# Order and size of loads around batch 1 of a sorted-block attention and its bilinear layer, with output tiles in halves

## The chip, the cores and the metric

One Trainium2 chip, one of its cores. The time is the device time of one execution in microseconds, as the median of several executions. Before the change it is 246.88 us (median of 3 runs, 246.43 to 246.95). A profile is taken from one further execution.

The engines have the profile's names: PE multiplies matrices (PEld loads its stationary operand), DVE and ACT work elementwise, POOL does that too and issues the loads, SP (SyncE) issues transposing DMAs and stores. All of them run their own list of instructions in order and wait for each other through semaphores.

## The reference

Four batches, eight heads, 768 positions, head size 64, blocks of 96 positions (8 blocks). Weights: 512 x 1536 twice and 1536 x 512. Inputs and output are float32.

```python
P = sort_net                                   # (4, 8, 8, 8)
for _ in range(5):
    P = exp(P - max(P, -1));  P = P / sum(P, -1);  P = P / sum(P, -2)
k_sorted = einsum('bhij,bhjcd->bhicd', P, k_blocks)
v_sorted = einsum('bhij,bhjcd->bhicd', P, v_blocks)
attn = softmax(q_blocks @ k_sorted^T / 8)      # inside each block
x = (attn @ v_sorted) -> (3072, 512)           # heads side by side
out = ((x @ w_a) * (x @ w_b)) @ w_out          # (3072, 512)
```

## The kernel before

**Units of work.** A *pair* is two heads of one batch; pairs 0 to 3 are batch 0, 4 to 7 batch 1, 8 to 11 batch 2, 12 to 15 batch 3. For each pair, k and v of all blocks are mixed by P (`pair_mix`, tiles kT and vT), v is turned by a transposing DMA of SP (`turn_v`, tile vs), q is brought into order by POOL (`pair_q`, tile qc, two buffers) and turned by a DMA of SP (`turn_q`, tile qTf, three buffers). Then come the scores and their exponential (`pair_scores`, tile eT), and the output of attention with its scaling on DVE (`pair_o` with `one_o`, tile xp), which SP turns into xT, the input of the bilinear layer. Batch 0 is done in another way, in two halves and with PE's own transposes, to begin early.

**The bilinear layer.** For each batch `ffn_ab(b, m, t)` computes one of 12 strips m of 128 columns for one half t of the batch's positions: four products with w_a, four with w_b, a copy by ACT, and the elementwise product by DVE into hT. Then `ffn_out(b, c)` computes one of six output tiles of 128 rows: 12 products with w_out into one PSUM tile, a copy by ACT or DVE, a store by SP.

**How they are laid between each other.** PE works on the bilinear layer of batch b, and the attention of batch b+1 lies between its steps. `units_full(b+1)` gives 12 units in the order M0 M1 R0 M2 R1 O0 M3 R2 O1 R3 O2 O3, where M is mixing and turning, R the scores and O the output of a pair. `interleave` runs the steps and after each of them as many units as keep up with the steps' count; an output tile counts as two steps (`outs`). The manual schedule keeps every engine's instructions in the order in which this program issues them.

**PSUM.** The attention's tiles (mix, sc, o_ps) share the two buffers of psA, the bilinear layer's (pf, po) the four of psF.

**The loads.** All loads are issued by POOL into one queue, cast from float32 to bfloat16 on the way; one issue takes POOL about 0.73 us. An issue waits until the load eight places earlier has landed. The order before is: q of batch 0, k and v of pairs 0 to 3, six chunks of 256 columns of w_a and w_b (`load_ab`), pairs 4 and 5, three chunks of w_out, pairs 6 and 7. A pair's load is three DMAs (k, v, q; 192 KB each as written). Between them POOL spreads P into the form that the mixing takes (`spread`, 2.0 us for a batch's heads) and copies pair 4's q. Pairs 8 and 9 are loaded in `pair_o` of pairs 6 and 7 (L311 to L316), pairs 10 and 11 in M of pairs 8 and 9 (L420), pairs 12 to 15 in `pair_o` of pairs 8 to 11. The pairs' tiles have six buffers (`ld`), so that pair 8 takes those of pair 2.

**SP's queue.** It carries the turns and the stores in program order. Around the end of batch 0 that is: turns of q and v of pairs 4 to 7 alternating, xT of pair 4, v of pair 7, then stores of output tile 0, xT of pair 5, stores of tile 1, xT of pair 6, stores of tile 2, q of pair 8, xT of pair 7, stores of tiles 3 to 5.

The steps of the prediction touch L108 to L117 (loads of weights), L263 to L272 (`pair_q`, `turn_q`), L309 to L323 (`pair_o`), L372 to L379 (`ffn_out`), L415 to L440 (`units_full`, `interleave`), and L551 to L572 (the order of the loads and the first two stretches of steps).

Of the kernel before, what the change touches and what calls it, by code (L numbers as in the profile page):

```python
# [9 lines left out]
FP32 = mybir.dt.float32  # L10
BF16 = mybir.dt.bfloat16
# [11 lines left out]
def kernel(  # L23
# [11 lines left out]
    nc = tc.nc  # L35
    P = 128
    B, H, S, D = q.shape
# [3 lines left out]
    DMODEL = H * D  # L41
# [4 lines left out]
    NCH = S // P  # L46
    HP = H // 2
    NPAIR = B * HP
    KA = DMODEL // P
    KO = DFF // P  # L50
    KH = KO // 2
# [6 lines left out]
    V0 = 16  # L58
    W = NCH * D
    HW = S // 2  # L60
    WC = 256
    NBUF = 3
    PSUM = bass.MemoryType.PSUM
    ET = mybir.EngineType
# [1 line left out]
    const = ctx.enter_context(tc.tile_pool(name="const", bufs=1))  # L66
# [5 lines left out]
    outp = ctx.enter_context(tc.tile_pool(name="outp", bufs=1))  # L72
    psA = ctx.enter_context(tc.tile_pool(name="psA", bufs=2, space=PSUM))
    psF = ctx.enter_context(tc.tile_pool(name="psF", bufs=4, space=PSUM))
# [18 lines left out]
    def load_pair(g):  # L93
        base = 2 * g * S * D
        tiles = []
        for name, t in (("k2", k), ("v2", v), ("q2", q)):
            if g < HP and name == "q2":
                continue
            to = ld.tile([P, 2, W], BF16, tag=name, name=name)
            nc.gpsimd.dma_start(out=to, in_=_ap(t, base, [[W, P], [S * D, 2], [1, W]]))  # L100
            tiles.append(to)
        loaded[g] = tiles
# [3 lines left out]
    w_out_sb = const.tile([P, KO, DMODEL], BF16, name="w_out_sb")  # L106

    def load_ab(c):  # L108
        for w_ap, w_sb in ((moe_w_a, w_a_sb), (moe_w_b, w_b_sb)):
            nc.gpsimd.dma_start(  # L110
                out=w_sb[:, :, c * WC:(c + 1) * WC],
                in_=w_ap.rearrange("(kc p) n -> p kc n", p=P)[:, :, c * WC:(c + 1) * WC])

    def load_out(c):
        nc.gpsimd.dma_start(
            out=w_out_sb[:, c * 4:(c + 1) * 4, :],
            in_=moe_w_out.rearrange("(kc p) n -> p kc n", p=P)[:, c * 4:(c + 1) * 4, :])  # L117
# [6 lines left out]
    for c in range(2):  # L124
        load_ab(c)
# [4 lines left out]
    kTs = [const.tile([P, S + PAD], BF16, name=f"kT{n}") for n in range(NBUF)]  # L130
# [23 lines left out]
    p_col = const.tile([P, NB, BH], BF16, name="p_col")  # L154

    def spread(eng, src, h0, n, i0=0, ni=NB):
        eng.tensor_tensor(
            out=s_all[:, h0:h0 + n, i0:i0 + ni],
            in0=_ap(mask, 0, [[CG, P], [0, n], [0, ni], [1, CG]]),
            in1=_ap(src, i0 * BH + h0, [[NB * BH, P], [1, n], [BH, ni], [0, CG]]),  # L160
            op=ALU.mult)

    def copy(eng, out, in_):
        if eng == "act":
            nc.scalar.copy(out=out, in_=in_)  # L165
        else:
            nc.vector.tensor_copy(out=out, in_=in_)  # L167
# [92 lines left out]

    def pair_q(g):  # L263
        qc = qtp.tile([P, NCH, 2, D], BF16, tag="qc", name="qc", bufs=2)
        nc.gpsimd.tensor_copy(out=qc.rearrange("p c e d -> p e c d"),  # L265
                              in_=loaded[g][2].rearrange("p e (c d) -> p e c d", c=NCH))
        st[g, "qc"] = qc

    def turn_q(g):
        qT = qtp.tile([P, NCH, P], BF16, tag="qTf", name="qTf", bufs=3)  # L270
        nc.sync.dma_start_transpose(out=qT, in_=st[g, "qc"].rearrange("p c e d -> p (c e d)"))
        st[g, "qT"] = qT  # L272
# [35 lines left out]

    def pair_o(g):  # L309
        xp = att.tile([BLK, NB, 2, D], BF16, tag="xp", name="xp")  # L310
        if g == 2 * HP - 2:  # L311
            load_pair(2 * HP)
        elif g == 2 * HP - 1:
            load_pair(2 * HP + 1)
            pair_q(2 * HP)
            turn_q(2 * HP)  # L316
        elif g >= 2 * HP and g + HP < NPAIR:
            load_pair(g + HP)
        for hf in range(2):
            one_o(eTs[g % NBUF], hf, vss[g % NBUF], hf * NBH, xp, NB)  # L320
        nc.sync.dma_start_transpose(
            out=xT_of(g // HP)[:, g % HP, :].rearrange("p (i t) -> p i t", i=NB),
            in_=xp.rearrange("p i e d -> p (i e d)"))  # L323

    hTs = {}
# [32 lines left out]
    def store(b, c, o):  # L360
        if b == 0:
            h, u = divmod(c, 3)
            for c2 in range(2):
                nc.sync.dma_start(
                    out=_ap(out, (h * PH * NCH + 2 * u + c2) * DMODEL,
                            [[NCH * DMODEL, PH], [1, DMODEL]]),
                    in_=o[c2 * PH:(c2 + 1) * PH])
        else:
            rows = out[b * S:(b + 1) * S, :].rearrange("(p c) n -> c p n", c=NCH)
            nc.sync.dma_start(out=rows[c], in_=o)  # L370

    def ffn_out(b, c):  # L372
        po = psF.tile([P, DMODEL], FP32, tag="F", name="po")
        for m in range(KO):
            nc.tensor.matmul(po, lhsT=hTs[b][:, m, c * P:(c + 1) * P], rhs=w_out_sb[:, m, :],  # L375
                             start=(m == 0), stop=(m == KO - 1))
        o_sb = outp.tile([P, DMODEL], FP32, tag="o_sb", name="o_sb", bufs=3)
        copy("act" if c % 2 == 0 else "dve", o_sb, po)
        store(b, c, o_sb)  # L379

    def ffn_out_cut(b, c, cut):
        rows = out[b * S:(b + 1) * S, :].rearrange("(p c) n -> c p n", c=NCH)[c]
        for n0, n1, eng, queue in ((0, cut, "dve", nc.sync), (cut, DMODEL, "act", nc.scalar)):
            po = psF.tile([P, DMODEL], FP32, tag="F", name="po")
            for m in range(KO):
                nc.tensor.matmul(po[:, 0:n1 - n0], lhsT=hTs[b][:, m, c * P:(c + 1) * P],  # L386
                                 rhs=w_out_sb[:, m, n0:n1],
                                 start=(m == 0), stop=(m == KO - 1))
            o_sb = outp.tile([P, n1 - n0], FP32, tag=f"o_cut{n0}", name="o_cut")
            copy(eng, o_sb, po[:, 0:n1 - n0])  # L390
            queue.dma_start(out=rows[:, n0:n1], in_=o_sb)
# [23 lines left out]
    def units_full(b):  # L415
        def M(g):
            pair_mix(g, "k", ("act", "act"))
            pair_mix(g, "v", ("dve", "act"))
            turn_v(g)
            if g in (2 * HP, 2 * HP + 1):  # L420
                load_pair(g + 2)
            if g + 1 < NPAIR and g + 1 != 2 * HP:
                pair_q(g + 1)
                turn_q(g + 1)

        g0 = b * HP
        order = [("M", 0), ("M", 1), ("R", 0), ("M", 2), ("R", 1), ("O", 0), ("M", 3),
                 ("R", 2), ("O", 1), ("R", 3), ("O", 2), ("O", 3)]
        what = {"M": M, "R": pair_scores, "O": pair_o}
        return [lambda w=w, n=n: what[w](g0 + n) for w, n in order]  # L430

    def interleave(steps, units, spare, slow=0, outs=0):
        n, done, at = len(steps), 0, 0
        for s, step in enumerate(steps):
            step()
            at += 1 if s < n - outs else 2
            want = s + 1 if s < slow else -(-at * len(units) // (n + outs - spare))
            while done < min(want, len(units)):
                units[done]()
                done += 1  # L440

    with tc.manual_schedule(engines={ET.PE, ET.Pool, ET.SP, ET.Activation, ET.DVE}):
        if True:
# [22 lines left out]
            for it in range(5):  # L466
                rsum, csum = chain[0][it], chain[1][it]
                nc.scalar.activation(out=p_nat, in_=p_nat, func=AF.Exp)
                if it == 2:
                    with nc.allow_low_precision("sum of one one and zeros"):  # L470
                        nc.vector.reduce_sum(
                            out=mask, in_=_ap(ident, 0, [[P, P], [1, CG], [CG, NB]]),
# [14 lines left out]
                else:  # L487
                    nc.vector.tensor_mul(
                        out=p_fin.bitcast(BF16).rearrange("h (i j u) -> h i j u", i=NB, j=NB),
# [58 lines left out]
                    half_x(0, 3, "act")  # L548
                ab_mms(begun[n], w_sb, 0, m, 0, range(KA - 1))

        load_ab(4)  # L551
        load_ab(5)
        load_pair(4)
        spread(nc.gpsimd, p_col, 8, 8)
        load_pair(5)
        for c in range(3):
            load_out(c)
        load_pair(6)
        pair_q(HP)
        turn_q(HP)  # L560
        load_pair(7)
        for n in range(2, 4):
            spread(nc.gpsimd, p_col, n * 8, 8)

        steps = [lambda: ffn_ab(0, 0, 0, begun[0:2]), lambda: ffn_ab(0, 1, 0, begun[2:4]),
                 lambda: ffn_ab(0, 2, 0, begun[4:5])]
        steps += [lambda m=m: ffn_ab(0, m, 0) for m in range(3, KO)]
        interleave(steps, units_half(), 1, 3)

        steps = [lambda m=m: ffn_ab(0, m, 1) for m in range(KO)]  # L570
        steps += [lambda c=c: ffn_out(0, c) for c in range(NCH)]
        interleave(steps, units_full(1), 6, outs=NCH)  # L572

        for b in range(1, B):
            steps = [lambda m=m, t=t, b=b: ffn_ab(b, m, t)
                     for m in range(KO) for t in range(2)]
            steps += [lambda c=c, b=b: ffn_out(b, c) for c in range(NCH)]
            if b == B - 1:
                steps[-1] = lambda b=b: ffn_out_cut(b, NCH - 1, 3 * P)
            interleave(steps, units_full(b + 1) if b + 1 < B else [], 8, outs=NCH)  # L580


# [28 lines left out]
```

## Time and profile before

| | us |
|---|---|
| median of 3 runs (range) | 246.88 (246.43 to 246.95) |
| the profiled execution | 247.89 |
| its span, first to last instruction | 246.1 |
| PE busy in it | 234.1 |
| DVE, ACT, POOL busy | 108.9, 104.0, 61.2 |
| share of 16 DMA engines' span: loads (queue 0), SP's DMAs (queue 1) | 40.9%, 29.6% |

The granted clock of PE was full in the whole span (mean 1.000). The page's second part cuts the span into 40 slices and gives the busy share of each in tenths; the list of waits gives, for each engine and line, what it waited for with the total, the number of times and the longest; the chain of waits goes back from the last instruction to what released it. In the rows of the DMA queues stand the packets that began in a window, their megabytes as written, and the time they took as a share of 16 engines' time in the window (over 100% where an engine has several packets in flight).

Where batches lie: batch 0's second half of positions is at 45 to 66 us with most of batch 1's attention between its steps, batch 0's output tiles at 66 to 85, batch 1's layer at 85 to 142, and so on to the last output tile at 243.

### The profile page before, as it was taken

Reading aid. Unit: us, or ns where it says so; the run is one execution under the profiler, and the core shown is the slowest. Engines: PE = TensorE matmul, PEld = TensorE weight load, DVE = VectorE, ACT = ScalarE, POOL = GpSimd, SP = SyncE. Lnnn points to the kernel's source line nnn. Section 1 sums busy time; section 2 is a strip of 40 time slices with the busy share of each in tenths; the row PEclk is TensorE's granted clock in tenths of the full one; section 3 lists DMA queues with packets and bytes.
Section 4 is the critical chain, followed back from the end, with each engine's and each line's share of the span. In section 5 each row is a group of like instructions: output and inputs, shape, how many; then the busy total and the mean of one; then the engine's idle time right before and its main releaser. Section 6 shows DMA issues by size and latency. Waiting matters only on the chain.

```text
span 246.1 us, 5514 instructions
## 1 busy us (share of the span) xinstructions
PE 234.1 (95%) x2250; PEld 139.2 (57%) x2259; DVE 108.9 (44%) x255; ACT 104.0 (42%) x204; POOL 61.2 (25%) x82
## 2 busy tenths in 40 slices
PE   6799999998979979999999999999999999999994
PEld 6576666665545446666654465666654466665443
DVE  6774557534426144464652153363561244443110
ACT  3575754674630047546430056737420033333001
POOL 8876857616144014471100001000000000000000
PEclk9999999999999999999999999999999999999999
DMA  6999999999999979899714335312114210000132
GB/s 80 203 199 194 196 201 206 167 185 168 149 113 235 207 180 119 147 157 192 115 23 128 131 91 105 75 34 43 35 44 149 85 45 0 0 3 1 43 123 90
DMA packets 56585, 28.67 MB, mean 117 GB/s; under 512 B 33392, under 2 KB 53616, under 8 KB 56560
## 3 DMA queue, kind: packets, MB, share of 16 engines
q0 software_dynamic: 20944, 14.16, 40.9%
q1 hardware_dynamic: 35472, 14.11, 29.6%
q8 instruction: 17, 0.28, 0.5%
q14 instruction: 8, 0.07, 0.1%
q10 hardware_dynamic: 144, 0.07, 0.1%
HBM read 28.32 MB, written 6.29 MB: 141 GB/s over the span
## 4 chain that ended last, share of the span: by engine, by line
PE 85%; DMA 7%; DVE 4%; ACT 1%; issue 1%; SPq 0%; DVEq 0%
PE pf L336 48%; PE po L375 22%; DMA qTf<-qc 3%; PE mix L281 3%; PE o_ps L249 3%; DMA xT<-xp 3%; PE sc L301 2%; PE mixh L199 2%; PE po L386 1%; PE vs_ps L226 1%; PE xt_ps L240 1%; PE sc L214 1%; DMA p_nat<-in_sort_net_dram 1%; PE two L336 1%; DVE xp L255 1%
## 5 line engine op out<-in xcount | busy, mean ns | idle before, releaser
L357 DVE TENSOR_TENSOR hT<-a_sb,pf 128x384 bf16<-128x384 bf16 x95 | 52.6, 554 | 77.0 <-PE pf L336 45.3
L336 PE MATMUL pf<-xT,w_a_sb 128*128 128x384 bf16 x380 | 78.0, 327 | 1.6 <-DMA xT<-xp 1.6
L336 PE MATMUL pf<-xT,w_b_sb 128*128 128x384 bf16 x380 | 77.4, 326 | 0.0
L356 ACT CAST a_sb<-pf 128x384 bf16<-128x384 f32 x95 | 45.5, 479 | 60.2 <-PE pf L336 38.9
L375 PE MATMUL po<-w_out_sb,hT 128*128 128x512 bf16 x267 | 60.6, 379 | 0.5
L336 PEld LDWEIGHTS <-w_b_sb 128*128 128x128 bf16 x384 | 37.5, 98 | 27.0 <-issue 2.4
L336 PEld LDWEIGHTS <-w_a_sb 128*128 128x128 bf16 x384 | 34.7, 98 | 22.2
L375 PEld LDWEIGHTS <-hT 128*128 128x128 bf16 x276 | 26.5, 98 | 30.8
L265 POOL COPY qc<-q 128x768 bf16<-128x768 bf16 x12 | 9.9, 826 | 77.3 <-DMA qTf<-qc 58.4
L165 ACT COPY o_sb<-po 128x512 f32<-128x512 f32 x12 | 7.0, 586 | 50.2 <-PE po L375 35.4
L167 DVE COPY o_sb<-po 128x512 f32<-128x512 f32 x11 | 7.6, 692 | 38.8 <-PE po L375 24.6
L306 ACT ACTIVATE eT<-sc 96x768 bf16<-96x768 f32 x24 | 18.2, 802 | 6.2 <-PE sc L301 6.2
L255 DVE TENSOR_TENSOR xp<-o_ps,rec 96x512 bf16<-96x512 f32 x24 | 16.5, 686 | 0.8
L165 ACT CAST kT<-mix 128x384 bf16<-128x384 f32 x24 | 10.3, 482 | 6.7 <-PE mix L281 6.7
L100 POOL DMA_DIRECT2D v<-in_v_dram x16 | 11.7, 729 | 1.9 <-PE pf L336 0.6
L100 POOL DMA_DIRECT2D k<-in_k_dram x16 | 11.7, 728 | 1.2 <-DMA w_a_sb<-in_moe_w_a_dram 0.6
L249 PEld LDWEIGHTS <-eT 96*128 96x128 bf16 x256 | 10.4, 97 | 2.6
L249 PE MATMUL o_ps<-vs,eT 96*128 96x65 bf16 x256 | 11.2, 193 | 0.0
L100 POOL DMA_DIRECT2D q<-in_q_dram x12 | 8.8, 734 | 1.9 <-DMA w_out_sb<-in_moe_w_out_dram 1.3
L253 DVE RECIPROCAL rec<-o_ps 96x8 f32<-96x8 f32 x32 | 6.3, 196 | 5.9 <-PE o_ps L249 5.9
L301 PE MATMUL sc<-qTf,kT 64*128 64x96 bf16 x192 | 6.3, 204 | 2.0 <-DVE xp L255 1.3
L301 PEld LDWEIGHTS <-kT 64*128 64x128 bf16 x192 | 4.5, 94 | 5.8 <-issue 3.2
(76 smaller groups left out, 147.6 us busy)
## 6 DMA issues: line engine op xcount, KB each, us to landing
out_dram<-o_sb SPq DMA_DIRECT2D x17, 256.0 KB, 2.0
k<-in_k_dram POOLq DMA_DIRECT2D x16, 192.0 KB, 7.8
v<-in_v_dram POOLq DMA_DIRECT2D x16, 192.0 KB, 8.1
q<-in_q_dram POOLq DMA_DIRECT2D x12, 192.0 KB, 9.0
w_a_sb<-in_moe_w_a_dram POOLq DMA_DIRECT2D x6, 256.0 KB, 9.8
w_b_sb<-in_moe_w_b_dram POOLq DMA_DIRECT2D x6, 256.0 KB, 10.1
w_out_sb<-in_moe_w_out_dram POOLq DMA_DIRECT2D x3, 512.0 KB, 12.3
out_dram<-o_sb SPq DMA_DIRECT2D x12, 128.0 KB, 4.3
```

The lines of the kernel that those rows point to most:

```text
L100: nc.gpsimd.dma_start(out=to, in_=_ap(t, base, [[W, P], [S * D, 2], [1, W]]))
L165: nc.scalar.copy(out=out, in_=in_)
L167: nc.vector.tensor_copy(out=out, in_=in_)
L249: nc.tensor.matmul(o_ps[:, e, i * (D + 1):(i + 1) * (D + 1)], lhsT=eT[:, hf, e, i * BLK:i * BLK + P], rhs=vs[0:BLK, i0 + i, V0 - 1 + e * ( ...
L255: nc.vector.tensor_tensor(out=_ap(xp, i0 * 2 * D, [[nxp * 2 * D, BLK], [D, 2], [2 * D, NBH], [1, D]]), in0=_ap(o_ps, 1, [[1024, BLK], [511 ...
L265: nc.gpsimd.tensor_copy(out=qc.rearrange("p c e d -> p e c d"), in_=loaded[g][2].rearrange("p e (c d) -> p e c d", c=NCH))
L301: nc.tensor.matmul(sc[:, e, i * BLK:(i + 1) * BLK], lhsT=kT[e * D:(e + 1) * D, blk * BLK:blk * BLK + P], rhs=qT[e * D:(e + 1) * D, :, blk ...
L306: nc.scalar.activation(out=eT[:, hf, :, 0:HB], in_=sc[0:BLK, :, 0:HB], func=AF.Exp, scale=float(scale))
L336: nc.tensor.matmul(pf[:, 0:HW], lhsT=w_sb[:, kc, m * P:(m + 1) * P], rhs=x_cols(b, kc, t), start=(kc == 0), stop=(kc == KA - 1))
L356: nc.scalar.copy(out=a_sb, in_=pf[:, 0:HW])
L357: nc.vector.tensor_mul(out=hT[:, m, t * HW:(t + 1) * HW], in0=a_sb, in1=ab[1][:, 0:HW])
L375: nc.tensor.matmul(po, lhsT=hTs[b][:, m, c * P:(c + 1) * P], rhs=w_out_sb[:, m, :], start=(m == 0), stop=(m == KO - 1))
```

## The change

1. The weights' columns are loaded in chunks of 256, 256, 512 and 512 (the first two before, the last two where the third and fourth were); the fifth and sixth chunk go.
2. The three chunks of w_out are loaded after pairs 6 and 7, not before them.
3. The spreads of P for batches 2 and 3 move from before the stretch into M of pairs 5 and 7.
4. Pairs 8 and 9 are loaded in M of pairs 6 and 7, which on POOL stand right after w_out.
5. Pairs 10 and 11 are held: POOL first copies one element (`hold`) of xp of pair 7, or of kT of pair 8, and issues the load after it.
6. q of pair 8 is copied and turned in `pair_o` of pair 5, not of pair 7. The loads in `pair_o` come after its output and turn.
7. Each output tile is two steps of six products; the weight of two steps for a whole tile (`outs`) goes. The last tile of all stays as it was.

As the program issues them, PE's instructions then differ in one stretch alone, batch 0's output tiles: pair 5's O stands after the first half of tile 0, pair 7's R after its second half, pair 6's O after tile 1, and pair 7's O after the first half of tile 2. Before, pair 5's O and pair 7's R both stood after tile 0, pair 6's O after tile 1, pair 7's O after tile 2. SP's order becomes: xT of pair 5, q of pair 8, stores of tiles 0 and 1, xT of pairs 6 and 7, stores of tiles 2 to 5.

```diff
-    WC = 256
+    AB = (0, 256, 512, 1024, 1536)
...
-                out=w_sb[:, :, c * WC:(c + 1) * WC],
-                in_=w_ap.rearrange("(kc p) n -> p kc n", p=P)[:, :, c * WC:(c + 1) * WC])
+                out=w_sb[:, :, AB[c]:AB[c + 1]],
+                in_=w_ap.rearrange("(kc p) n -> p kc n", p=P)[:, :, AB[c]:AB[c + 1]])
...
+    held = const.tile([1, 1], BF16, name="held")
+
+    def hold(of):
+        nc.gpsimd.tensor_copy(out=held, in_=of)
...
     def pair_o(g):
         xp = att.tile([BLK, NB, 2, D], BF16, tag="xp", name="xp")
-        if g == 2 * HP - 2:
-            load_pair(2 * HP)
-        elif g == 2 * HP - 1:
-            load_pair(2 * HP + 1)
-            pair_q(2 * HP)
-            turn_q(2 * HP)
-        elif g >= 2 * HP and g + HP < NPAIR:
-            load_pair(g + HP)
...
+        if g == HP + 1:
+            pair_q(2 * HP)
+            turn_q(2 * HP)
+        if g == 2 * HP - 1:
+            hold(xp[0:1, 0, 0, 0:1])
+            load_pair(2 * HP + 2)
+        elif g >= 2 * HP and g + HP < NPAIR:
+            load_pair(g + HP)
...
-        po = psF.tile([P, DMODEL], FP32, tag="F", name="po")
-        for m in range(KO):
-            nc.tensor.matmul(po, ...)
+        def part1():
+            v["po"] = psF.tile([P, DMODEL], FP32, tag="F", name="po")
+            mms(range(KH))
+
+        def part2():
+            mms(range(KH, KO))
...
-            if g in (2 * HP, 2 * HP + 1):
+            if g in (HP + 2, HP + 3):
                 load_pair(g + 2)
+            if g == 2 * HP:
+                hold(kTs[g % NBUF][0:1, 0:1])
+                load_pair(g + 3)
+            if g in (HP + 1, HP + 3):
+                spread(nc.gpsimd, p_col, (g - HP + 3) // 2 * 8, 8)
...
-        load_ab(4)
-        load_ab(5)
         load_pair(4)
         spread(nc.gpsimd, p_col, 8, 8)
         load_pair(5)
-        for c in range(3):
-            load_out(c)
         load_pair(6)
         pair_q(HP)
         turn_q(HP)
         load_pair(7)
-        for n in range(2, 4):
-            spread(nc.gpsimd, p_col, n * 8, 8)
+        for c in range(3):
+            load_out(c)
```

More of the change, by code (lines that the diff above doesn't have):

```diff
@@ L372, in ffn_out, with mms @@
     def ffn_out(b, c):
-        po = psF.tile([P, DMODEL], FP32, tag="F", name="po")
-        for m in range(KO):
[L375 to L379, printed above, removed]
+        v = {}
+        def mms(ms):
+            for m in ms:
+                nc.tensor.matmul(v["po"], lhsT=hTs[b][:, m, c * P:(c + 1) * P],
+                                 rhs=w_out_sb[:, m, :], start=(m == 0), stop=(m == KO - 1))
+        def part1():
[3 more added lines that the diff above has]
+            mms(range(KH, KO))
+            o_sb = outp.tile([P, DMODEL], FP32, tag="o_sb", name="o_sb", bufs=3)
+            copy("act" if c % 2 == 0 else "dve", o_sb, v["po"])
+            store(b, c, o_sb)
+        return [part1, part2]
     def ffn_out_cut(b, c, cut):
@@ L430, in units_full, with interleave @@
         return [lambda w=w, n=n: what[w](g0 + n) for w, n in order]
-    def interleave(steps, units, spare, slow=0, outs=0):
-        n, done, at = len(steps), 0, 0
+    def interleave(steps, units, spare, slow=0):
+        n, done = len(steps), 0
         for s, step in enumerate(steps):
             step()
-            at += 1 if s < n - outs else 2
-            want = s + 1 if s < slow else -(-at * len(units) // (n + outs - spare))
+            want = s + 1 if s < slow else -(-(s + 1) * len(units) // (n - spare))
             while done < min(want, len(units)):
@@ L570 @@
         steps = [lambda m=m: ffn_ab(0, m, 1) for m in range(KO)]
-        steps += [lambda c=c: ffn_out(0, c) for c in range(NCH)]
-        interleave(steps, units_full(1), 6, outs=NCH)
+        steps += [part for c in range(NCH) for part in ffn_out(0, c)]
+        interleave(steps, units_full(1), 6)
         for b in range(1, B):
@@ L576 @@
                      for m in range(KO) for t in range(2)]
-            steps += [lambda c=c, b=b: ffn_out(b, c) for c in range(NCH)]
+            steps += [part for c in range(NCH - (b == B - 1)) for part in ffn_out(b, c)]
             if b == B - 1:
-                steps[-1] = lambda b=b: ffn_out_cut(b, NCH - 1, 3 * P)
-            interleave(steps, units_full(b + 1) if b + 1 < B else [], 8, outs=NCH)
+                steps.append(lambda b=b: ffn_out_cut(b, NCH - 1, 3 * P))
+            interleave(steps, units_full(b + 1) if b + 1 < B else [], 8)
 _INS = ['q', 'k', 'v', 'sort_net', 'moe_w_a', 'moe_w_b', 'moe_w_out']
```

## The prediction

> **What bounds the kernel now.** I read the page first, then TensorE's waits, then the chain of waits from 44 to 92 us, and last the two DMA queues in short windows of that stretch.
>
> ```profile
> PE 234.1 (95%) x2250; PEld 139.2 (57%) x2259; DVE 108.9 (44%) x255; ACT 104.0 (42%) x204; POOL 61.2 (25%) x82
> PE   6799999998979979999999999999999999999994
> DMA  6999999999999979899714335312114210000132
> ```
>
> TensorE (PE) is busy for 234.1 of 246.1 us and its slices of 6.15 us are full from the sixteenth (92 us) to the last but one, so after that there is nothing that a schedule can win. The holes are at both ends, which the change leaves alone, and in the tenth, twelfth and fifteenth slice (55 to 92 us). The DMA row is nearly full until there. PE's own waits there:
>
> ```profile
> PE pf L336 <- DMA xT<-xp: 1.6, 1, 1.6
> PE sc L301 <- DVE xp L255: 1.3, 2, 0.8
> PE sc L301 <- DMA qTf<-qc: 0.8, 1, 0.8
> ```
>
> 3.7 us in three places; that is the most that the change can win. The chain of waits (start, length, what) places them:
>
> ```profile
> 48.62 8.47 DMA qTf<-qc
> 57.09 0.14 issue
> 57.23 0.52 PE sc L301 x16
> ...
> 68.88 0.26 PE o_ps L249 x8
> ...
> 70.24 0.70 DVE xp L255
> ...
> 70.98 0.34 PE sc L301 x8
> ...
> 80.94 6.49 DMA xT<-xp
> 87.48 0.97 PE pf L336 x5
> ```
>
> Wait A: the scores of pair 5 (57.23) stand 0.77 us for the turn of pair 5's q. Wait B: the scores of pair 7 (70.15 and 70.98) stand 0.77 + 0.49 us because pair 5's output step went right before them and holds both psA buffers until VectorE has scaled it. Wait C: batch 1's first product stands 1.62 us for the turn of pair 7's xp.
>
> The turns are DMAs of SyncE (queue 1); the loads are POOL's (queue 0). The lines below are queue rows (packets, MB, share of 16 engines) of the windows 20-22, 39-42, 49-51, 51.5-53.5 (two rows), 59-60, 44.5-46 (two rows), in this order:
>
> ```profile
> q0 software_dynamic: 784, 0.39, 144.8%
> ...
> q0 software_dynamic: 622, 0.62, 124.4%
> ...
> q0 software_dynamic: 555, 0.40, 131.2%
> ...
> q0 software_dynamic: 386, 0.28, 90.2%
> q1 hardware_dynamic: 385, 0.10, 36.5%
> ...
> q1 hardware_dynamic: 1068, 0.27, 126.2%
> ...
> q0 software_dynamic: 127, 0.13, 99.8%
> q1 hardware_dynamic: 121, 0.03, 55.0%
> ```
>
> Alone, queue 0 moves 0.20 MB a us and queue 1 1068 packets a us. Together they alternate packet for packet, 193 a us each: a turn of q or x (768 packets of 256 bytes) takes 4.0 us instead of 0.7 while loads are queued. And from 44.5 to 46 both nearly stop, after a load of code at 43.7. Loads of code at 26.9 and 34.1, with no turn in flight, show no such pause; those at 56.9, 69.9 and 81.2, with turns in flight, are followed by one of about 1 us each.
>
> **The change, part by part.** The order of PE's instructions differs in one place only, the first four output tiles of batch 0; ACT's and DVE's orders are the same. The whole effect thus lies in the three waits, or in new ones.
>
> *Half tiles (wait B).* After the change pair 5's output step comes after 6 of the 12 products of tile 0, and 6 more stand between it and pair 7's scores. In the chain the second psA buffer came free 70.98 - 68.68 = 2.30 us after the output step began. Now PE has the step (0.49), 6 products at 2.59/12 = 0.216 (1.30), 0.11 for entering a new group (7 products after scores took 1.62, not 1.51) and the first scores (0.23): 2.13. Left are 0.17 of waiting and 0.11 for the added boundary: 1.26 becomes 0.28, a gain of 1.0. Worst case 0.5, if pair 7's turn of q, which took 10.4 us from issue to landing, is late here; before, it had two pairs' loads beside it, after, one.
>
> *Pairs 10 and 11 held, pair 8's q turned early, half tiles (wait C).* Before, the last turn of xp was issued at 80.94, though xp was ready at 79.15: SyncE was issuing pair 8's turn of q (79.16, 1.69) that stood ahead of it. It landed 10.5 us after pair 7's output step began (76.94), and 8.9 were to be had. Now pair 8's turn is ahead of tiles 0 and 1's stores, and that step comes 6 products earlier against the rest: 0.49 + 42 x 0.216 + 0.11 + 3 x 0.163 = 10.1 us. The turn is issued 2.3 after the step begins. It takes 2.8 us (the fastest turn of q, alone), 6.5 (its own row) or 9.0 (pair 6's): landing at 5.1, 8.8 or 11.3, a wait of 0, 0 or 1.2. Pair 10's loads do not go away: the hold releases them once xp's first half is written, 1.5 us after the step begins, so they start beside this very turn. I take 0.3, a gain of 1.3 (0.4 to 1.6). The early turn makes SyncE wait for POOL's copy of pair 8's q, with the stores and turns of tiles 0 and 1, pairs 6 and 7 queued behind; POOL reaches it some 64 us in (after pair 5's turn lands: a copy 0.8, three issues 2.2, a spread 2.0, a copy 0.8), SyncE at 71: 7 us of cover.
>
> *w_out behind pairs 6 and 7, pair 8 right behind it (wait A).* The bytes up to w_out and pair 7 are the same, so their end stays near 55.5, where queue 0 ran dry before. What is new is pair 8. POOL issues it once pair 4's turn of q has landed (two qc buffers; 49.5 before, earlier now), so it stands in queue 0 with no gap: 3 x 256 packets, 768/193 = 4.0 us more of alternation, and the turns of pair 4's v and pair 5's q (1024 + 768 packets, issued at 47.34 and 48.62, behind the same vT as before) have to live with it. Before, they ended in the gap after 55.5. Credits: (a) wider chunks move 2.1 MB at 0.207 MB a us (the window 39-42 row, 1 KB packets) instead of 0.196: 0.57 us or 0.115 MB, 150 of pair 8's packets, 0.8 us. (b) Pair 4's turn of q lies beside 768-byte packets instead of 1 KB ones (146 a us at 43-44): some 0.075 MB less is held up, 0.5 us. (c) That turn now starts about 2 us earlier and is through by 44.6, so the pause of 44.5 finds no turn: 1.5 us at 0.20 instead of 0.13 MB, 0.17 MB, 1.15 us. Left: 4.0 - 0.8 - 0.5 - 1.15 = 1.55 us longer. In that time queue 1 has 300 of its own packets moved (0.28 us alone): the turn lands 1.3 later, at 58.4, and wait A grows by 1.3. Upper bound: no credits (4.0 less 0.7, 3.3) and a pause at 57.4 on the unfinished turn (1.0): 4.3. Lower bound: pair 8 comes too late to matter and the credits stand: the wait is gone, -0.8. I take +1.3, nearest to the rows of this stretch.
>
> [...] The trace has 0.196 against 0.207, which is why I keep (a).
>
> *Costed at nothing.* Wide chunks land later as wholes: the b half of the first by 27.5 (its last narrow part before), needed at 30.3. w_out lands near 54, needed at 66.1; were that cover gone, each us would count. Spreads (2.0 each) move into POOL's idle stretches. The hold before pair 11 keeps POOL until kT of pair 8 (90); behind it pair 9's q has until 103.4. Pairs 12 to 15 come up to 4 us later; the next to use one is batch 3, at 141.7.
>
> **Sum.** -1.0 (B) - 1.3 (C) + 1.3 (A) = -1.0, rounded down to -0.9 for small boundaries. The profiled span of 246.1 becomes 245.2, with the 1.8 around it 247.0. The profiled execution took 247.89, the median of the runs is 246.88; against the median: 246.0.
>
> **Rivals.** *Pair 8 holds up the turns (slower).* One mechanism, at wait A: for it speak the alternation row and the three pauses that met turns; against it, credits (a) to (c). Without (c) and with the pause at 57.4: (4.0 - 1.3) x 0.82 (1.3 of 1.55, as above) + 1.0 = 3.2, so 3.2 - 1.0 - 1.2 = +1.0: 247.9; without any credit +2.0: 248.9. It decides from a landing of 59.9 on. *The pause alone (no change):* credits stand, the pause strikes: 2.3 - 1.0 - 1.3 = 0: 246.9. Measured, 0.2% (0.5 us) either way can't be told from no change. *Pair 8 comes late:* wait A vanishes, 246.9 - 0.8 - 2.3 = 243.8; against it: pair 4's turn has to land before 51.0 for its own scores.
>
> **How the numbers follow.** Forecast 0.39, late pair 8 0.07, the pause alone 0.18, held up 0.36. The first two are faster by over 0.2%: 0.46; same 0.18; slower 0.36. The forecast's own range is 245.0 to 246.4 (A between +0.5 and +1.7). The range for 8 in 10: 244.5 (a little of the late-pair case) to 248.5 (most of the slower one).
>
> **What would show it.** Wait B under 0.4; wait C under 0.5; pair 5's turn of q landing at 58.4, and pair 8's loads issued before 50. A landing past 59.9 makes the forecast wrong and the slower rival right; a wait for w_out, or PE waits after 92 us, would be something that I have not seen.

## The result, and the profile after

| | before | after |
|---|---|---|
| median of 4 runs each (range) | 246.91 (246.43 to 247.18) | 250.83 (249.89 to 251.4) |
| ratio, 95% interval | | 1.0157 [1.0122, 1.0192] |
| profiled execution | 247.89 | 250.68 |
| its span | 246.1 | 248.9 |
| mean granted clock of PE | 1.000 | 0.986 |

The changed kernel is slower by 1.6%, 3.9 us. The forecast (246.0) is wrong, and 250.83 lies 2.3 us above the end of the range, 248.5. Here and below a median is that of all runs, and a ratio leaves out single slow runs, those over 1.5% above their kernel's fastest.

First the page of the changed kernel: PE's busy time, its 40 slices of 6.2 us, and the clock that was granted to it in the same slices.

```profile
PE 237.9 (96%) x2250; PEld 141.6 (57%) x2259; DVE 109.0 (44%) x255; ACT 103.9 (42%) x204; POOL 58.7 (24%) x80
...
PE   7899999994999999999999999999999999999994
...
PEclk9999999996799999999999999999999999999999
```

PE is busy for 237.9 us where it was busy for 234.1, with the same 2250 matmuls. Most of that is work at a lower clock (2.64 of the 3.8 us, below), and the last row says where: slices ten and eleven, 56 to 68 us. It had a full clock everywhere before.

PE's waits (total, times, longest) that answer to the three of before:

```profile
PE sc L306 <- DMA qTf<-qc: 3.6, 1, 3.6
...
PE o_ps L249 <- DVE xp L255: 0.4, 1, 0.4
```

Wait B (scores of pair 7) and wait C (batch 1's first product) are gone, and a new one of 0.42 us stands at the output step of pair 7. Wait A, the turn of pair 5's q, went from 0.77 to 3.56. The chain of waits of the changed kernel, from 46 to 62 us (start, length, what):

```profile
48.60 11.26 DMA qTf<-qc
59.86 0.14 issue
60.00 0.82 PE sc L306 x16
60.82 1.39 PE pf L341 x4
```

The turn was issued when it was before (48.60 against 48.62) and took 11.26 us instead of 8.47. The two lines after it hold the second thing to see: 16 products of the scores took 0.82 us, and the same 16 took 0.52 before. The windows of the changed kernel (stretch, its length, busy time and count of PE, PEld, DVE, ACT and POOL, then PE's clock, the DMA share and GB/s) show when that began and ended:

```profile
58.00:60.00 2.00, 0.00 (x1) 0.03 (x2) 0.00 (x0) 0.00 (x0) 0.00 (x0) 0.61 1.17 196
60.00:62.00 2.00, 2.00 (x20) 1.19 (x21) 0.00 (x0) 1.46 (x2) 1.99 (x3) 0.50 1.17 238
62.00:64.00 2.00, 2.00 (x18) 1.32 (x17) 0.40 (x1) 0.52 (x2) 2.00 (x3) 0.50 0.88 76
64.00:66.00 2.00, 2.00 (x15) 1.17 (x13) 1.76 (x5) 0.37 (x1) 1.73 (x2) 0.68 1.46 161
```

PE went idle at 56.44. In the window 58 to 60 it did nothing and its clock averaged 0.61, so the clock fell to half inside that window; worked out from rows of half a microsecond (0.95 from 58.0 to 58.5, 0.50 after it), at 58.46. It came back at 65.28 (0.72 from 65.0 to 65.5, 1.00 after it). From 60.00 to 65.28 PE worked at half speed, 18 to 20 products in 2 us where f2 (below), at full clock, has 27 to 33 in the same stretch of work. Half of 5.28 us is lost: 2.64 us.

The account of the span, from the two profiles:

| | us |
|---|---|
| wait A, 0.77 to 3.56 | +2.79 |
| half clock, 5.28 us | +2.64 |
| wait B, 1.26 to 0 | -1.26 |
| wait C, 1.62 to 0 | -1.62 |
| new wait at pair 7's output step | +0.42 |
| sum | +2.97 |
| measured, 248.9 - 246.1 | +2.8 |

Why the turn took longer is in POOL's order. POOL's list of the kernel before (start, length, line, what; in brackets the idle time before and what ended it):

```profile
57.24 0.83 POOL L265 COPY qc<-q 128x768 bf16<-128x768 bf16 x1 [4.44 <-DMA qTf<-qc]
58.01 0.76 POOL L100 DMA_DIRECT2D k<-in_k_dram  x1
```

and of the changed kernel:

```profile
45.24 0.82 POOL L270 COPY qc<-q 128x768 bf16<-128x768 bf16 x1 [1.77 <-DMA qTf<-qc]
46.00 0.77 POOL L100 DMA_DIRECT2D k<-in_k_dram  x1
...
60.02 0.82 POOL L270 COPY qc<-q 128x768 bf16<-128x768 bf16 x1 [11.81 <-DMA qTf<-qc]
```

The copy of pair 7's q needs a buffer that pair 5's turn sets free, so before, POOL stood there until 57.24, just behind that turn's landing at 57.09, and the load of pair 8 (the k line after it) was behind it in the program. Nobody had written that as a gate, but it was one: pair 8 could not load while pair 5's q was being turned. The change puts the load ahead of that copy, and it is issued at 46.00, 12 us earlier. Rows of the two DMA queues of the changed kernel, in the windows 41.5-43.5, 54-56 and 57.45-58.2 (two rows each; packets, MB, share of 16 engines):

```profile
q0 software_dynamic: 271, 0.20, 99.1%
q1 hardware_dynamic: 288, 0.07, 65.9%
...
q0 software_dynamic: 389, 0.28, 89.6%
q1 hardware_dynamic: 393, 0.10, 37.1%
...
q1 hardware_dynamic: 41, 0.01, 26.7%
q0 software_dynamic: 6, 0.00, 3.4%
```

The middle pair is the alternation, still going on at 54 to 56 us, 195 packets a us for each, where queue 0 was about to run dry before. The last pair is a pause: 47 packets in 0.75 us. A pause stands in the trace of before too, from about 57.4 on (17 packets from 57.4 to 58.2), but there the turn had landed 0.3 us earlier; here it was caught by it. The first pair is a slower stretch on the turn of pair 4's q, which had been at 44.5 to 46 before: 271 packets of queue 0 in 2 us, where the undisturbed alternation of the middle pair has 389 of the same size. It is slower, not nearly at a stop as the pause of before was (9 packets of both queues from 45.0 to 45.5).

### The profile page after: what moved, and what is told of

The parts are those of the page before. It is cut to its first block, busy times and chain, and to the rows that moved or that the text cites. A ratio compares the mean times of both kernels' runs of the same rounds, so it can differ in the third digit from the quotient of the medians.

```text
span 248.9 us, 5511 instructions
## 1 busy us (share of the span) xinstructions
PE 237.9 (96%) x2250; PEld 141.6 (57%) x2259; DVE 109.0 (44%) x255; ACT 103.9 (42%) x204; POOL 58.7 (24%) x80
## 4 chain that ended last, share of the span: by engine, by line
PE 87%; DMA 5%; DVE 4%; ACT 1%; issue 1%; SPq 0%
PE pf L341 48%; PE po L382 23%; DMA qTf<-qc 5%; PE mix L286 3%; PE o_ps L249 3%; PE sc L306 2%; PE mixh L199 2%; PE po L402 1%; PE vs_ps L226 1%; PE xt_ps L240 1%; PE sc L214 1%; DMA p_nat<-in_sort_net_dram 1%; PE two L341 1%; DVE xp L255 1%; ACT p_nat L488 1%
## 5 line engine op out<-in xcount | busy, mean ns | idle before, releaser
L341 PE MATMUL pf<-xT,w_a_sb 128*128 128x384 bf16 x380 | 79.1, 330 | 0.0
L361 ACT CAST a_sb<-pf 128x384 bf16<-128x384 f32 x95 | 45.5, 479 | 60.6 <-PE pf L341 38.6
L249 PE MATMUL o_ps<-vs,eT 96*128 96x65 bf16 x256 | 11.8, 196 | 0.4 <-DVE xp L255 0.4
L171 PE MATMUL heat<-warm 128*128 128x128 bf16 x72 | 7.2, 280 | 1.3 <-DVE warm L84 1.3
```

Source lines behind the costliest of these rows:

```text
L249: nc.tensor.matmul(o_ps[:, e, i * (D + 1):(i + 1) * (D + 1)], lhsT=eT[:, hf, e, i * BLK:i * BLK + P], rhs=vs[0:BLK, i0 + i, V0 - 1 + e * ( ...
L341: nc.tensor.matmul(pf[:, 0:HW], lhsT=w_sb[:, kc, m * P:(m + 1) * P], rhs=x_cols(b, kc, t), start=(kc == 0), stop=(kc == KA - 1))
L361: nc.scalar.copy(out=a_sb, in_=pf[:, 0:HW])
```

## The experiments

Each kernel ran beside runs of the kernel before on the same chip; ratios are against those. Labels that begin with e ran on one chip (before: 246.77), f on a second (246.22), g on a third (246.45). Diffs are against the changed kernel unless another is named.

| run | edit | median (runs) | ratio, 95% |
|---|---|---|---|
| e1_p8_behind_q7 | pair 8's load back behind pair 7's copy | 245.76 (10) | 0.9958 [0.992, 0.9997] |
| g2_one_move | the same | 246.63 (10) | 0.9994 [0.9968, 1.0019] |
| e2_wout_first | w_out before pair 6 again | 247.7 (10) | 1.0026 [0.998, 1.0072] |
| f1_after_again | none | 252.46 (4) | 1.0224 [1.0163, 1.0284] |
| e3_fill | PE kept busy in wait A | 249.71 (4) | 1.0115 [1.0037, 1.0193] |
| f2_fill_again | the same | 248.77 (10) | 1.0081 [1.0045, 1.0117] |
| e4_half_alone | before, with half tiles only | 246.32 (10) | 0.9991 [0.9956, 1.0026] |
| g3_half_alone | the same | 246.47 (10) | 0.9985 [0.9945, 1.0025] |
| f3_whole_tiles | e1 with whole tiles | 247.71 (10) | 1.0024 [0.9983, 1.0065] |
| f4_later_loads | e1, and later loads, units over 19 steps | 243.96 (10) | 0.9906 [0.9871, 0.9941] |
| g4_best | the same | 243.92 (10) | 0.9917 [0.9889, 0.9946] |
| g1_p8_early | f4 with pair 8's load early | 249.05 (4) | 1.0128 [1.007, 1.0187] |

### Undo one step: pair 8's load (e1, g2)

```diff
-            if g in (HP + 2, HP + 3):
+            if g == HP + 3:
                 load_pair(g + 2)
...
                 pair_q(g + 1)
                 turn_q(g + 1)
+            if g == HP + 2:
+                load_pair(g + 2)
```

> The changed kernel with one line moved: POOL issues pair 8's load after its copy of pair 7's q (which waits for pair 5's turn), not before it. Theory (pair 8's packets in queue 0 hold up pair 5's turn of q; the 3.6 us of idle that follow halve PE's clock): pair 5's turn lands near 56.5 instead of 59.86, the scores of pair 5 wait less than 0.5 us, the clock stays at 1.0, and the kernel takes 243.5 to 245, faster than both. Rival 1 (w_out's larger packets beside the turns are what is slow): the turn still lands after 58.5 and the time stays above 248. Rival 2 (the drop of the clock has a cause of its own): the wait goes but the clock still drops for some 7 us near 58, time 246 to 248.

The chain of e1 and, after it, POOL's list of e1:

```profile
53.73 2.71 PE pf L341 x16
56.44 0.45 PE sc L306 x16
56.89 1.41 PE pf L341 x8
```

```profile
56.18 0.83 POOL L270 COPY qc<-q 128x768 bf16<-128x768 bf16 x1 [9.93 <-DMA qTf<-qc]
56.95 0.76 POOL L100 DMA_DIRECT2D k<-in_k_dram  x1
```

The chain stays on PE through 56.44, where the changed kernel left it for 3.56 us. POOL has pair 5's turn at 56.18 and loads pair 8 after it, and the clock is 1.00 in each window of 2 us from 56 to 64 (mean of the span 0.998). The span is 242.8, 6.1 less than the changed kernel's; wait A and the half clock are 3.56 + 2.64 = 6.2. (The profiled execution, 244.59, is the fastest of its ten; by the two ratios, on two chips, the kernels are 2.0% apart, some 5 us.) w_out stands where the change put it, so w_out's larger packets are not the cause. The median of 245.76 is a little above what was expected.

> The changed kernel with only pair 8's load behind pair 7's copy, again, for one chip's comparison: 244.5 to 245.8, below the kernel before and 0.5 to 1.5 us above the fastest.

The repeat on another chip gave 246.63, above what was expected and no different from before, and its profile has a wait A of 2.0 us at full clock. What this step alone is worth thus varies with the chip and the execution; that it takes the loss of the change away holds on both.

### Undo another: w_out (e2)

```diff
+        for c in range(3):
+            load_out(c)
         load_pair(6)
...
         load_pair(7)
-        for c in range(3):
-            load_out(c)
```

> The changed kernel with w_out loaded before pairs 6 and 7 again; pair 8 still follows the last of them with no gap. Theory: queue 0 holds the same bytes at 57, so pair 5's turn still lands after 59, the wait stays 2.5 us or more, the clock drops, time 249.5 to 251.5. Rival 1 (w_out's place): the turn lands by 57.5, the wait falls under 1.2 us, the clock stays at 1.0, time under 246.

PE's waits of e2, and POOL's list:

```profile
PE sc L306 <- DMA qTf<-qc: 2.8, 2, 2.1
```

```profile
52.06 0.82 POOL L270 COPY qc<-q 128x768 bf16<-128x768 bf16 x1 [6.28 <-DMA q<-in_q_dram]
52.83 0.76 POOL L100 DMA_DIRECT2D k<-in_k_dram  x1
```

The expectation's premise did not hold. With w_out ahead, pair 6's q lands at 51.95 instead of 41.47, POOL stands idle for 6.28 us until then, and pair 8 follows at 52.83; its first packets move near 57, when the rest of queue 0 is through (pair 7's q landed at 56.06). PE then waits only 0.71 for pair 5's turn, as before, and 2.08 for pair 6's, which was issued at 56.14 and meets pair 8. So steps 2 and 4 of the change act together: w_out behind the pairs brings pair 6's q early, and that lets POOL reach pair 8's load early. Undoing either one keeps pair 5's turn free of it.

### The clock by itself (f1, e3, f2)

The fill adds 15 products of a tile of zeros, 512 columns each, into pair 5's score tile, which the real scores overwrite. They run 3.40 us, in the time in which PE waits.

```diff
             sc = psA.tile([P, 2, 512], FP32, tag="A", name="sc")
+            if g == HP + 1 and hf == 0:
+                keep_busy(sc[:, 0], 15)
```

> The changed kernel with 15 products of zeros on PE right before pair 5's scores, into the same PSUM tile, overwritten by the scores (15 x 0.216 = 3.2 us, in the 3.6 us of waiting). Theory (idle PE costs its clock): pair 5's turn lands as late as before, 59.9, the clock stays at 1.0, and half of the 5.3 us that ran at half speed after the wait comes back: 2.6 us, time near 248.2. Rival 2 (a cause of its own): the clock drops all the same, time 250.5 to 251.

e3 gave 249.71. In its profile the turn landed at 62.1, 2.51 us of waiting were left behind the fill, and the clock stayed full. With the interval as wide as it was, it was repeated beside the unaltered kernel:

> The changed kernel, unaltered, beside the next one on the same chip. Theory: PE waits 2.5 to 5.5 us for pair 5's turn, its clock is at half for 5 to 8 us around it, time 249.5 to 251.5.

> The changed kernel with the 15 products of zeros before pair 5's scores once more, to set its time beside the unaltered one's. Theory (idle PE costs its clock): clock 1.0 in the trace, the turn as late as in the unaltered kernel, time 1.5 to 3 us below it. Rival (a cause of its own, or the clock not worth its half): within 1 us of it.

Windows of f1, with PE's clock third from the end:

```profile
62.00:64.00 2.00, 1.25 (x18) 0.92 (x19) 0.00 (x0) 0.71 (x2) 1.24 (x2) 0.50 1.24 253
64.00:66.00 2.00, 2.00 (x8) 0.91 (x6) 0.00 (x0) 1.27 (x3) 1.98 (x4) 0.50 0.86 101
```

and of f2:

```profile
62.00:64.00 2.00, 2.00 (x27) 1.35 (x24) 1.59 (x5) 0.79 (x2) 1.98 (x3) 1.00 0.87 85
64.00:66.00 2.00, 2.00 (x33) 1.27 (x32) 1.68 (x4) 0.92 (x3) 1.87 (x2) 1.00 1.45 174
```

The unaltered kernel has the half clock again, from 60.2 to 67.0, behind a wait of 4.59. With the fill the clock is full in all ten runs of f2 (in three of e3's four), though PE does 3.40 us more work, and the kernel is 252.46 - 248.77 = 3.7 us faster on the same chip. That more work makes it faster shows that the clock was a cost by itself. The size is above the expected 1.5 to 3: the half clock accounts for 2.1 in f1's profile (62.75 to 67.0, halved) and 2.64 in the first. f1's profiled execution, the slowest of its four, also began 1.7 us late, and its wait of 4.59 is 0.8 longer than the 3.40 + 0.38 of f2; whether its other runs differ so is not shown, and the rest of the 3.7 stays unexplained.

### Half tiles alone (e4, g3), and without them (f3)

```diff
 # the kernel before, with this part of the change:
...
-        steps += [lambda c=c: ffn_out(0, c) for c in range(NCH)]
-        interleave(steps, units_full(1), 6, outs=NCH)
+        steps += [part for c in range(NCH) for part in ffn_out(0, c)]
+        interleave(steps, units_full(1), 6)
...
```

> The kernel before with the half-tile steps alone. Theory: pair 7's scores no longer wait for VectorE (1.26 us before), pair 7's output step, now 1.3 us after pair 6's, waits about 0.4 us for it; the last turn of xp, issued earlier against the need, waits 0 to 1 us instead of 1.62: time 245.0 to 246.4. Rival (the half steps' extra boundaries and the new wait eat it): within 0.3 us of 246.9.

> The kernel before with the half-tile steps alone, again, for one chip's comparison. If the loads' new order has a worth of its own, beyond the half tiles, this one is 0.5 to 1.5 us above the changed kernel with the one move; if the half tiles are all of it, they are equal within 0.4 us.

PE's waits of e4:

```profile
PE o_ps L249 <- DVE xp L255: 0.4, 1, 0.4
PE sc L301 <- DMA qTf<-qc: 0.2, 1, 0.2
```

Wait B is gone, and so is wait C; the 0.4 us at pair 7's output step is there, so it comes from the half tiles (the output steps of pairs 6 and 7 are six products apart and share psA). The profiles' spans, 243.1 and 243.5, are 2.6 to 3.0 below that of before, yet the medians are level with it: 246.32 and 246.47, ratios whose intervals hold 1. e4's profiled execution, 244.84, was the fastest of its ten, and that of before, 247.89, was 1 us above its median; g3's, 246.39, is at its median, but 2.9 us of it lie outside its span, against 1.8 for before. One execution's profile is not the median. By the intervals the half tiles gain at most 1.1 us (e4) and 1.4 us (g3), not the 2.5 that the profiles show at waits B and C less the 0.42.

> The kernel with pair 8's load behind pair 7's copy, with whole output tiles as before the change (the holds, the early turn of pair 8's q and the loads' order stay). Theory (the half tiles end the second wait and give the last turn of xp 1.3 us, the holds and the early turn give it little): pair 7's scores wait about 1.2 us for VectorE again, batch 1's first product waits 0 to 1 us, time 1 to 2 us above the kernel with half tiles. Rival (the holds and the early turn alone cure the last turn's wait, half tiles only the scores' one): the first product waits 0.0, time 0.8 to 1.2 us above it.

PE's waits of f3:

```profile
PE sc L306 <- DMA qTf<-qc: 3.4, 1, 3.4
PE sc L306 <- DVE xp L255: 1.3, 2, 0.8
```

With whole tiles wait B is back at its old 1.3 us, and wait C is not, so the held loads and the early turn of pair 8's q end it by themselves. Either half of the change was enough for C in these traces. f3's median is 0.7% above e1's by the ratios, about B's size, but the intervals overlap. (Its profiled execution, 250.81, is 3 us above its median; only B, C and, in the last section, the clock are read from it.)

### A version that beats both (f4, g4), and the step put back into it (g1)

f4 takes e1, spreads the units of the first stretch over 19 steps instead of 18, so that pair 7's output step comes half a tile later, and gives pairs 10 and 11 one load each behind kT of pairs 8 and 9 instead of the hold on xp.

```diff
-        if g == 2 * HP - 1:
-            hold(xp[0:1, 0, 0, 0:1])
-            load_pair(2 * HP + 2)
-        elif g >= 2 * HP and g + HP < NPAIR:
+        if g >= 2 * HP and g + HP < NPAIR:
             load_pair(g + HP)
...
-            if g in (HP + 2, HP + 3):
+            if g == HP + 3:
                 load_pair(g + 2)
-            if g == 2 * HP:
+            if g in (2 * HP, 2 * HP + 1):
                 hold(kTs[g % NBUF][0:1, 0:1])
-                load_pair(g + 3)
+                load_pair(g + 2)
...
+            if g == HP + 2:
+                load_pair(g + 2)
...
-        interleave(steps, units_full(1), 6)
+        interleave(steps, units_full(1), 5)
```

> The kernel with pair 8's load behind pair 7's copy, and two more steps: the units of the first stretch at 12/19 of the steps instead of 12/18 (pair 7's output step then stands a whole tile after pair 6's), and pairs 10 and 11 held until kT of pair 8 and of pair 9. Expected: the 0.42 us wait of the output step for VectorE goes; the last turn of xp is issued about 1.3 us later against its need and now runs without loads beside it, so that it lands 3 us after its issue and nothing waits for it; time 0.3 to 0.5 us below the kernel with the one move. If the turn is late all the same, a wait of up to 1 us shows at batch 1's first product and the time is above.

> The fastest kernel so far, again: 243.5 to 244.5; in an undisturbed profile no wait of PE from 55 to 92 us over 0.5 us.

g1 is g4 with the line of e1 taken back: pair 8's load ahead of pair 7's copy.

> The fastest kernel so far (pair 8's load behind pair 7's copy, units at 12/19, pairs 10 and 11 held until kT of pairs 8 and 9) with that one load put back ahead of the copy. Theory (this place of pair 8's load is what costs): pair 5's turn lands 2.5 to 5 us later than in the kernel without the step, PE's clock halves for 3 to 7 us, time 5 to 8 us above it on the same chip. Rival (the other steps of the change or the chip's spread made the difference): within 2 us of it.

PE's waits of g4, and after it of g1:

```profile
PE sc L306 <- DMA qTf<-qc: 1.7, 1, 1.7
...
PE xt_ps L240 <- DVE xph L255: 0.4, 1, 0.4
```

```profile
PE sc L306 <- DMA qTf<-qc: 3.0, 1, 3.0
```

f4 and g4 are 0.9% and 0.8% faster than before on two chips, and g4 is further below the kernel with the one move (246.63 on that chip) than the expected 0.3 to 0.5 us; the new wait at pair 7's output step is not among g4's waits. What was missed: a wait A under 0.5 was expected, and both profiles show one (1.9 and 1.7). Six of g4's ten runs took 243.7 to 244.0 against 245.51 for the profiled one, less by about as much as that wait; whether they had none is not shown.

g1 costs 249.05 - 243.92 = 5.1 us for one moved load, in a kernel that is otherwise the same. Its clock was 0.993 in three of four runs and 0.979 in the profiled one (251.23, 2 us above the others), where it is half from 60.2 to 67.0; that alone would give a mean of 0.986, so by the mean some 3.6 us elsewhere were at half too, an estimate. The rival, under which pair 8's place costs less than 2 us, falls.

## Why the prediction was wrong, and where it was right

**Two steps failed: the size of wait A, and the clock, which was put at nothing.** "I take +1.3" was mis-sized: wait A measured +2.79. What was subtracted from 4.0 us were three credits, together worth 2.45 x 0.82 = 2.0 us of the turn's landing. e1 shows them without pair 8 in the way: there pair 5's turn landed at 56.03, 1.06 earlier than before. (In g2 it landed at 58.26, so this is one pair of executions.) What is short, 0.95, is what (c) was put at, 1.15 x 0.82 = 0.94: "so the pause of 44.5 finds no turn: 1.5 us at 0.20 instead of 0.13 MB". From 44.5 to 46 queue 0 did move 0.29 MB, but the slower stretch at 41.5 lay on the turn that had been moved earlier too. And another pause, which had missed pair 5's turn by 0.3 us before, met the longer turn for some 0.65 us at 57.5. Without (c) the prediction's own working gives (4.0 - 1.3) x 0.82 = 2.2; with that pause 2.9. Measured: 2.79. That it is (c) and not another credit is read from the traces, not tried. The alternation and the place were right; the slower rival had them too, and was held less likely because of the credits.

**The clock.** Every case priced wait A by its own length, up to 4.3 us more. In the four profiles with a wait of 3.01 to 4.59 us PE's clock was halved too, which cost 2.64 us more in the changed kernel. This is the larger miss: the landing, 59.86, was just short of the 59.9 that was to make the forecast wrong, and wait A at its measured size gives by the prediction's sum about 247.4, inside the range. That is why the slower rival, right in place and mechanism, was also too cheap (247.9 to 248.9 against 250.83), and why the range ended too low.

**The base of the sum.** The forecast took 0.9 us off the median for waits read from a profiled execution that was 1.0 us above it. The spans moved by 2.8 us, the medians by 3.9. In the traces waits B and C went about as forecast, but in the medians the half tiles alone, which end both, show no gain (e4, g3). Where the median execution of the kernel before spends what its profile spends in B and C is open.

**Wait B** was predicted to fall from 1.26 to 0.28. It fell to 0, and 0.42 came back at pair 7's output step, which the working did not look at: the step's two neighbours share psA just as the scores did. Net 0.84 for 1.0.

**Wait C** was predicted at 0.3, and is 0. The gain of 1.62 needed only one of the two edits it was put down to.

**Costed at nothing.** No wait for w_out, none after 92 us that was not there before, pair 8's loads before 50 (46.00), and POOL's copy of pair 8's q at 64.88 for the 64 that was worked out: all as written.

**The pauses follow loads of code:** this does not hold throughout. In the changed kernel the slower stretch of 41.5 came ahead of the loads of code at 44.3 and 46.0, and in f1 the rows of one from 41.5 to 46 show no load of code; the pause of 57.5 did follow one, at 56.3. What starts them is open; no run here tried it.

**What stays open.** The loads' new order was not worth anything measurable beside the half tiles (g2 246.63, g3 246.47). g4 is 2.7 us below g2 by the median of the same chip, of which the traces name 0.42 at pair 7's output step and 0.3 at wait A; its two steps were not tried apart.

## What to carry to other kernels

An instruction that waits in an engine's program order is a gate for every transfer issued behind it, as POOL's copy at 57.24 was for pair 8's load at 58.01: before moving a load ahead of such an instruction, name what was in flight while it waited. A wait of PE can have a price beyond its length (here waits of 3.01 to 4.59 us had one, those of 1.92 to 2.51 had none), so a slower case has to be costed with the clock, and filling the wait with products that are overwritten is worth a trial (3.7 us here). A credit that rests on a stall staying at its time is the first to be doubted when everything around it moves.

## What the runs showed of the hardware that was not expected

Behind the four longest of the waits below PE's clock was at half. The waits for a turn of q that eight profiles show, and the clock (us; the half stretches from rows of half a microsecond, otherwise the mean over the span):

| run | wait | from, to | clock |
|---|---|---|---|
| f1 | 4.59 | 58.16 to 62.75 | half from 60.2 to 67.0 |
| after | 3.56 | 56.44 to 60.00 | half from 58.5 to 65.3 |
| f3 | 3.36 | 56.89 to 60.25 | half from 61.4 to 64.9 |
| g1 | 3.01 | 57.95 to 60.96 | half from 60.2 to 67.0 |
| e3 | 2.51 | 59.65 to 62.16 | mean 1.000 |
| e2 | 2.08 | 64.57 to 66.65 | mean 1.000 |
| g2 | 2.01 | 56.39 to 58.40 | mean 1.000 |
| f4 | 1.92 | 56.41 to 58.33 | mean 1.000 |

In f1, after and g1 the clock fell while PE still waited; in f3 it fell 1.2 us after the wait had ended. What sets the moment of the fall or of the return is not shown, nor what a wait between 2.51 and 3.01 us would have done. The loss beyond the wait, estimated as half of the time that PE worked at half clock, was 1.7 us (f3, 61.4 to 64.9) to some 3 us (g1, 60.96 to 67.0).

Both DMA queues slowed down or nearly stopped in places while turns were in flight: 47 packets in 0.75 us in the changed kernel (57.45 to 58.2), 17 in 0.8 us before (57.4 to 58.2), and in f1 from 43.5 to 46 only 221 packets of the loads and 59 of the turns in 2.5 us, where the changed kernel's alternation has 389 and 393 in 2 us. They are not at the same time in every execution of the same kernel (the turn of pair 5's q took 11.26 us in one profile and 12.30 in the other), which is why one profile of such a stretch is not its time.
